# Agent attention with a gated convolution on one core: the 49th agent's weight written as one minus the other 48

## The chip, the cores and the metric

The kernel runs on one NeuronCore of a Trainium2 chip. The metric is device time in microseconds (us) of one execution, the median of several runs. The core has five engines that run side by side, each through its own list of instructions in order: TensorE (PE, matrix products; PEld is its loading of weights), VectorE (DVE), ScalarE (ACT), GpSimd (POOL) and SyncE (SP). In this kernel SP issues every DMA but one.

## What is computed

Four batches of 12800 tokens with 128 channels, and 49 agents in each batch:

```python
a2k = softmax(scale * agents @ k.T); agent_v = a2k @ v        # 49 x 128
q2a = softmax(scale * q @ agents.T);  x = q2a @ agent_v       # 12800 x 128
gate = sigmoid(sum over 5 taps of conv_w[k] * x shifted by 4 - k tokens)   # zeros ahead of a batch
out = (gate * (x @ w_val)) @ w_out
```

Every row of `q2a` holds 49 weights that add up to one. The inputs are random, and the agents, q, k and the convolution's weights are scaled up.

## The kernel before

The tokens are taken in units of 1280; a batch has ten, and `g` counts all forty. Two units are a segment (`s` from 0 to 19), and 512 tokens are a chunk (`t` from 0 to 100, five to a segment). x itself is never formed: its product with `agent_v`, `conv_w` and `w_val` is folded into weights (`wst`, turned into `stat`) that act on the agents' softmax weights directly. For precision each weight and each softmax value is split into a 16-bit high part and a 16-bit rest, so that a product is three products: high by high, rest by high, high by rest.

**A query unit** (`queries`) goes through eight steps: scores on PE, a transpose (L400) and a maximum (L757) on DVE, the subtraction on POOL (L762), the exponential on ACT (L770), the sum and its reciprocal on DVE, the weights times 256 on DVE (L781), and then the 128 columns of the tile `pt`: the high parts by ACT (L789), a second copy of a third of the weights by POOL (L795, two instructions), and the rests by POOL (L803). There are four buffers `pt`, unit g uses buffer g modulo 4. The tile is turned by a DMA transpose (L844, SP) into rows of `x1`: 49 rows of rests, 49 rows of high parts, and 30 rows that repeat the high parts of 30 agents. The first four units are turned on PE instead.

**The third product** (high value by rest of the weight) needs each of 49 agents once more: 30 have their second copy in `x1`, and 19 are left over. For those, `shifts` (L893) copies rows of `x1` into `x2`, five times each, each copy one token further, so that all five taps of the convolution are one matrix product with 95 rows. It does that with two DMAs for a segment: 16 rows (80 rows of `x2`) and 3 rows (15 rows of `x2`). The first two segments go by single units.

**A chunk** has three parts on PE: the gate (`gates`: five products with `x1`, L931, one with `x2`, L935), the value (`values`: L958 and L962) and the output (`project`: L1003 to L1005). ACT takes the tanh (L944), DVE multiplies (L971), ACT and POOL split the result (L979, L984), ACT scales the output (L1024), SP stores two chunks at a time (L1039).

**The fold of a batch** (`fold_weights`) makes the weights from the agents' values in five steps, each a PE piece with DVE, POOL and ACT work around it: `avT` (L548 to L550) is the normalised agents' values, `gw` the same times the taps (L555), `wst` the split weights (L599 to L658), and PE's transposes of them (L669) give `stat`. The first batch's fold splits the gate's weights on ACT and POOL (L647, L636), the others on DVE (L627, L599).

**What sets the order.** PE's order is a string written out by hand (g, a and o are a chunk's gate, value and output; q, k, v, t and f the units and folds). The other engines and the DMA queue are ordered by a planner (`Plan.order`), which simulates the kernel with an estimated duration for each step and issues the steps by their simulated starts. A changed estimate or a removed step can therefore move instructions on ACT, DVE, POOL and SP. SP is one queue in order: an issue that waits for its data holds all issues behind it.

Of the kernel before, what the change touches and what calls it, by code (L numbers as in the profile page):

```python
# [31 lines left out]

NDUP = 30
THIRDS = 16
X2R = 19
LAST = 42
X2CUTS = ((0, THIRDS, 1, 3, 0.5), (THIRDS, X2R, LAST, 3, 0.2))

# [152 lines left out]
def tile_agent_attention_gated_conv(  # L191
# [335 lines left out]
    def fold_weights(b):  # L527
# [55 lines left out]

        x2g = wst[:, TAPS + 1, 0 : TAPS * X2R].rearrange("p (r k) -> p k r", k=TAPS)
        x2v = wst[:, TAPS + 2, 0 : TAPS * X2R].rearrange("p (r k) -> p k r", k=TAPS)
        ghi = wst[:, 0:TAPS, 0:A]
        vhi = wst[:, TAPS, 0:A]

        def thirds(x, first, end):
            return x[..., first:end:3]  # L590

        def lows(low, full, hi, less):


            for out, first, end in zip(low, (2, 0, 1, LAST), (A, LAST, A, A)):
                less(out, thirds(full, first, end), thirds(hi, first, end))

        def rest(out, full, s, hi):
            dve.scalar_tensor_tensor(  # L599
                out=out, in0=full, scalar=rs[:, s : s + 1], in1=hi,  # L600
                op0=ALU.mult, op1=ALU.subtract,
            )

        def val_weights():
            dve.tensor_reduce(
                out=mx[:, 1:2], in_=pv[:, 0:A], axis=AX.X, op=ALU.max,
                apply_absolute_value=True,
            )
# [6 lines left out]
            low = (  # L615
                wst[:, TAPS, 2 * A : 2 * A + THIRDS], wst[:, TAPS, 2 * A + THIRDS :],
                x2v[:, HALO, 0:THIRDS], x2v[:, HALO, THIRDS:],
            )
            lows(low, pv[:, 0:A], vhi, lambda out, full, hi: rest(out, full, 1, hi))

        gate_lows = (
            wst[:, 0:TAPS, 2 * A : 2 * A + THIRDS], wst[:, 0:TAPS, 2 * A + THIRDS :],
            x2g[:, :, 0:THIRDS], x2g[:, :, THIRDS:],
        )

        def gate_weights():
            dve.tensor_scalar_mul(ghi, gw, rs[:, 0:1])  # L627

# [5 lines left out]
        def gate_rest_pool():  # L634
            def less(out, full, hi):
                nc.gpsimd.tensor_tensor(out=out, in0=full, in1=hi, op=ALU.subtract)  # L636

            lows(gate_lows, gs, ghi, less)

        def gate_rest():  # L640
            lows(gate_lows, gw, ghi, lambda out, full, hi: rest(out, full, 0, hi))
# [10 lines left out]
        add(  # L652
            "act", 0.4,
            lambda: nc.scalar.copy(out=wst[:, 0:TAPS, A : 2 * A], in_=ghi),
            [(*w_, "g")], [(*w_, "d")],
        )
        add(
            "act", 0.22, lambda: nc.scalar.copy(out=wst[:, TAPS, A : 2 * A], in_=vhi),  # L658
            [(*w_, "v")], [(*w_, "e")],
# [83 lines left out]
    def queries(b, u):  # L743
# [30 lines left out]
        def sums():  # L774
# [47 lines left out]
    def halo(s):  # L822
# [9 lines left out]

        read.append(("x2", (s - 1) % 3, UNIT, 0))
        add("pool", 0.19, fn, read, [("x1h", s % NX)])

    def transposes(b, u):
# [36 lines left out]
        shifts(b, u)  # L873

    def shifts(b, u):

# [22 lines left out]
        if g % 2 and (g + 1) // 2 < B * NU // 2:
# [7 lines left out]
    def gates(t):  # L907
# [15 lines left out]
        xs = row_keys(segs_[0], halves_)  # L923
        x2k = [("x2", segs_[0] % 3, h, c[0]) for h in halves for c in X2CUTS]
# [26 lines left out]
    def values(t):  # L951
# [5 lines left out]
        def matmuls():  # L957
# [246 lines left out]
```

## Time and profile before

| | before |
|---|---|
| time, median of 3 runs | 419.22 us (417.06 to 420.21) |
| profiled execution, its span | 417.7 us |
| PE busy | 398.0 us, 95% |
| ACT, DVE, POOL busy | 299.7, 288.7, 243.2 us |
| moved by DMA | 127.64 MB, mean 306 GB/s |
| chain that ended last | PE 86%, DMA 5%, DVE 4%, ACT 2%, issue 1% |

The profile is of one execution more. Its own time is known as its span, from the first to the last instruction. PE's matrix products overlap and their ends are modelled, so PE's busy share says when it had work, not how well it was used; the chain of waits follows the work that ended last back from the end, and shows the pace (0.22 us for a product of 512 columns).

### The profile page before, as it was taken

Reading aid. Unit: us, or ns where it says so; the run is one execution under the profiler, and the core shown is the slowest. Engines: PE = TensorE matmul, PEld = TensorE weight load, DVE = VectorE, ACT = ScalarE, POOL = GpSimd, SP = SyncE. Lnnn points to the kernel's source line nnn. Section 1 sums busy time; section 2 is a strip of 40 time slices with the busy share of each in tenths; the row PEclk is TensorE's granted clock in tenths of the full one; section 3 lists DMA queues with packets and bytes.
Section 4 is the critical chain, followed back from the end, with each engine's and each line's share of the span. In section 5 each row is a group of like instructions: output and inputs, shape, how many; then the busy total and the mean of one; then the engine's idle time right before and its main releaser. Section 6 shows DMA issues by size and latency. Waiting matters only on the chain.

```text
span 417.7 us, 10023 instructions
## 1 busy us (share of the span) xinstructions
PE 398.0 (95%) x3905; PEld 197.6 (47%) x3905; DVE 288.7 (69%) x529; ACT 299.7 (72%) x519; POOL 243.2 (58%) x301
## 2 busy tenths in 40 slices
PE   4859999999899999999999999999999999999996
PEld 1329634446545544345546544444564544444443
DVE  3967798957747765684896876895689598745222
ACT  0647457798785767778787686788869577887775
POOL 1410447864656626656378585564178869968552
PEclk9988999999999999999999999999999999999999
DMA  8999999999999999999999999999999998974733
GB/s 314 421 416 412 370 372 318 296 351 280 303 346 315 326 297 371 259 296 371 332 355 310 275 327 346 324 315 341 316 388 288 290 316 205 268 199 143 202 128 127
DMA packets 75132, 127.64 MB, mean 306 GB/s; under 512 B 50467, under 2 KB 50851, under 8 KB 75085
## 3 DMA queue, kind: packets, MB, share of 16 engines
q1 hardware_dynamic: 74940, 126.87, 96.7%
q8 instruction: 31, 0.51, 0.5%
q10 hardware_dynamic: 144, 0.13, 0.2%
q14 instruction: 17, 0.13, 0.1%
HBM read 79.25 MB, written 26.21 MB: 253 GB/s over the span
## 4 chain that ended last, share of the span: by engine, by line
PE 86%; DMA 5%; DVE 4%; ACT 2%; issue 1%; POOL 0%; SPq 0%; DVEq 0%; ACTq 0%
PE gate L931 25%; PE sc L390 19%; PE av L494 11%; PE val L958 5%; PE out L1003 5%; DMA ld<-kT 5%; PE gate L935 5%; PE val L962 5%; PE out L1004 5%; PE out L1005 5%; ACT ob L1024 1%; PE sc L858 1%; DVE wst L599 1%; DVE h L971 1%; DVE qmx L757 0%
## 5 line engine op out<-in xcount | busy, mean ns | idle before, releaser
L984 POOL TENSOR_TENSOR hl<-h,hh 128x512 f16<-128x512 f32 x99 | 117.2, 1185 | 98.5 <-ACT hh L979 97.7
L931 PE MATMUL gate<-x,stat 128*128 128x512 f16 (+1 forms) x500 | 124.2, 378 | 0.0
L971 DVE SCALAR_TENSOR_TENSOR h<-th,val 128x512 f32<-128x512 f32 x100 | 68.0, 680 | 69.3 <-PE val L962 33.2
L390 PE MATMUL sc<-ld,ag_sb 128*32 128x320 f32 x1280 | 99.8, 448 | 8.9 <-DMA ld<-qT 6.1
L944 ACT ACTIVATE th<-gate,unscale 128x512 f32<-128x512 f32 x100 | 68.5, 685 | 21.6 <-PE gate L935 20.1
L979 ACT CAST hh<-h 128x512 f16<-128x512 f32 x99 | 60.9, 616 | 25.4 <-DVE h L971 24.5
L1024 ACT ACTIVATE ob<-out,oscale 128x512 f32<-128x512 f32 x98 | 67.4, 687 | 15.0 <-PE out L1005 14.5
L931 PEld LDWEIGHTS <-stat 128*128 128x128 f16 x505 | 48.2, 98 | 60.2 <-issue 4.8
L762 POOL TENSOR_TENSOR qw<-sT,qmx 128x490 f32<-128x490 f32 x40 | 43.0, 1076 | 41.8 <-DVE qmx L757 41.6
L390 PEld LDWEIGHTS sc<-ld,ag_sb 128*32 128x32 f32 x1280 | 38.5, 112 | 56.9 <-issue 20.0
L494 PE MATMUL av<-ld,eT 128*32 128x129 f32 (+1 forms) x1400 | 50.7, 277 | 1.7 <-DVE eT L400 1.1
L494 PEld LDWEIGHTS av<-ld,eT 128*32 128x32 f32 (+1 forms) x1400 | 45.8, 115 | 10.0 <-issue 2.9
L803 POOL TENSOR_TENSOR pt<-qw,pt 128x490 f16<-128x490 f32 x40 | 44.9, 1124 | 2.7 <-ACT pt L789 2.6
L400 DVE STREAM_TRANSPOSE sT<-sc 128x640 f32<-128x640 f32 x40 | 33.6, 843 | 16.3 <-PE sc L390 15.5
L485 ACT ACTIVATE e<-ks,kbias 128x320 f32<-128x320 f32 x80 | 39.4, 553 | 5.6 <-DVE kbias L471 2.7
L400 DVE STREAM_TRANSPOSE eT<-e 128x640 f32<-128x640 f32 x40 | 33.0, 833 | 14.2 <-ACT e L485 8.6
L795 POOL TENSOR_SCALAR pt<-qw 128x160 f16<-128x160 f32 x80 | 31.9, 418 | 16.4 <-DVE qw L781 16.4
L416 ACT COPY ks<-sc 128x640 f32<-128x640 f32 x40 | 27.6, 693 | 19.2 <-PE sc L390 17.3
L958 PE MATMUL val<-x,stat 128*128 128x512 f16 x100 | 38.0, 380 | 0.9 <-DVE wo L738 0.6
L1003 PE MATMUL out<-hh,wo 128*128 128x512 f16 x98 | 37.3, 380 | 1.0 <-ACT ob L1024 0.8
L935 PE MATMUL gate<-x,stat 95*128 95x512 f16 x100 | 38.0, 380 | 0.0
L962 PE MATMUL val<-x,stat 95*128 95x512 f16 x100 | 38.0, 380 | 0.0
(132 smaller groups left out, 401.6 us busy)
## 6 DMA issues: line engine op xcount, KB each, us to landing
ld<-qT SPq DMA_DIRECT2D x40, 640.0 KB, 10.8
ld<-kT SPq DMA_DIRECT2D x40, 640.0 KB, 8.1
ld<-vP SPq DMA_DIRECT2D x39, 645.0 KB, 7.3
outT<-ob SPq DMA_DIRECT2D x48, 512.0 KB, 6.4
x<-x SPq DMA_DIRECT2D x18, 400.0 KB, 8.2
x<-x SPq DMA_DIRECT2D x18, 75.0 KB
x<-x SPq DMA_DIRECT2D x4, 200.0 KB, 5.6
outT<-ob SPq DMA_DIRECT2D x3, 256.0 KB
```

Source lines behind the costliest of these rows:

```text
L390: nc.tensor.matmul(out=out[g * BLK : (g + 1) * BLK, j, 0:GT], lhsT=ag_sb[:, b, j * BLK : (j + 1) * BLK], rhs=src[:, g * GT : (g + 1) * GT] ...
L400: nc.vector.transpose(out=out.rearrange("p n (j i) -> p j n i", j=2), in_=in_.rearrange("p j (n i) -> p j n i", i=BLK),)
L494: nc.tensor.matmul(out=av[o + j : o + j + cols, 0 : C + 1], lhsT=et[:, n, j : j + cols], rhs=vt[:, n, :], start=(u == 0 and n < 2), stop=( ...
L931: nc.tensor.matmul(out=pg, lhsT=stat[:, k, :], rhs=x1[:, c : c + w], start=(k == 0), stop=False,)
L935: nc.tensor.matmul(out=pg, lhsT=stat[0 : TAPS * X2R, TAPS + 1, :], rhs=x2[0 : TAPS * X2R, o2 : o2 + w], start=False, stop=True,)
L944: lambda: nc.scalar.activation(out=th, in_=pg, func=AF.Tanh, scale=unscale[:, 0:1]),
L958: nc.tensor.matmul(out=pv, lhsT=stat[:, TAPS, :], rhs=x1s[(b * NCH + n0 // CH) // 5 % NX][:, PAD + o2 : PAD + o2 + w], start=True, stop=False,
L962: nc.tensor.matmul(out=pv, lhsT=stat[0 : TAPS * X2R, TAPS + 2, :], rhs=x2[0 : TAPS * X2R, o2 : o2 + w], start=False, stop=True,)
L971: lambda: nc.vector.scalar_tensor_tensor(out=h, in0=th, scalar=1.0, in1=pv, op0=ALU.add, op1=ALU.mult),
L979: "act", 0.18 + 0.43 * scale, lambda: nc.scalar.copy(out=hh, in_=h),
L984: lambda: nc.gpsimd.tensor_tensor(out=hl, in0=h, in1=hh, op=ALU.subtract),
L1024: lambda: nc.scalar.activation(out=ob[:, o : o + w], in_=po, func=AF.Copy, scale=oscale if w == CH else 1.0),
```

## The change

The softmax weights of a token add up to one, so the 49th is one minus the other 48. The changed kernel subtracts the 49th agent's value from the other 48 (a new DVE instruction in the fold) and adds the 49th agent's value times a constant one. 48 agents split evenly: 32 have their second copy in `x1` (two times 16, where it was 16 and 14), and 16 are left for `x2`, so one DMA for a segment does it and the one of three rows is gone (22 DMAs in all). The constant is ten rows of `x2` (rows 96 to 105, two for each tap: high part and rest of the weight) that hold 256, the scale of the weights. The rows are written once, at the start, by two POOL memsets and one DVE memset of 64 rows by 2560. Ahead of a batch a tap must see zero instead of one: a small tile `edge` holds the pattern, and `ones_edge` copies it into the first four columns when a segment starts a batch, and writes 256 back when the buffer is used again. The product with `x2` has 106 rows where it had 95. POOL's and ACT's tiles have 48 columns a block instead of 49.

```diff
-X2CUTS = ((0, THIRDS, 1, 3, 0.5), (THIRDS, X2R, LAST, 3, 0.2))
+R = 3 * THIRDS
+ONES = 96
+X2K = ONES + 2 * TAPS
...
+    edge = const.tile([P, HALO], F16, name="edge")
+    nc.gpsimd.memset(edge, QS)
+    nc.gpsimd.affine_select(
+        out=edge, in_=edge, pattern=[[2, HALO]], compare_op=ALU.is_ge, fill=0.0,
+        base=-ONES - 2 * HALO, channel_multiplier=1,
+    )
...
+    for t in x2s[0:2]:
+        nc.gpsimd.memset(t[AP_:, :], QS)
+    nc.vector.memset(x2s[2][AP_:, :], QS)
...
             dve.tensor_tensor(out=avT, in0=pt[:, AP_ : AP_ + A], in1=den, op=ALU.mult)
-
-        add("dve", 0.95, normalise, [at_t], ["avT"])
+            dve.tensor_scalar(
+                out=avT[:, 0:R], in0=avT[:, 0:R], scalar1=avT[:, R:A], scalar2=None,
+                op0=ALU.subtract,
+            )
+
+        add("dve", 1.05, normalise, [at_t], ["avT"])
...
-            dve.tensor_scalar_mul(vhi, pv[:, 0:A], rs[:, 1:2])
+            dve.tensor_scalar_mul(vhi, pv[:, 0:R], rs[:, 1:2])
+            dve.tensor_scalar_mul(ones_v[:, 0:1], pv[:, R:A], rs[:, 1:2])
...
         def gate_weights():
-            dve.tensor_scalar_mul(ghi, gw, rs[:, 0:1])
+            dve.tensor_scalar_mul(ghi, gw[:, :, 0:R], rs[:, 0:1])
+            dve.tensor_scalar_mul(ones_g[:, :, 0:1], gw[:, :, R:A], rs[:, 0:1])
...
-            add("act", 0.4, lambda: nc.scalar.copy(out=ghi, in_=gs), ["gs"], [(*w_, "g")])
+
+            def gate_highs():
+                nc.scalar.copy(out=ghi, in_=gs[:, :, 0:R])
+                nc.scalar.copy(out=ones_g[:, :, 0:1], in_=gs[:, :, R:A])
+
+            add("act", 0.62, gate_highs, ["gs"], [(*w_, "g")])
...
+    def ones_edge(s):
+        pairs = NU // 2
+        at = x2s[s % 3][ONES:, 0:HALO]
+        if s % pairs == 0:
+            add("pool", 0.1, lambda: nc.gpsimd.tensor_copy(out=at, in_=edge[ONES:, :]), (), [("x2e", s % 3)])
+        elif s >= 3 and (s - 3) % pairs == 0:
+            add("pool", 0.1, lambda: nc.gpsimd.memset(at, QS), (), [("x2e", s % 3)])
...
-        for r0, r1, first, every, us in X2CUTS:
-            first += A
-            rows = x1[first : first + 1 + (r1 - r0 - 1) * every : every, c : c + 1]
...
+        rows = x1[R + 1 : 2 * R : 3, c : c + 1]
+        view = [rows.ap[0], (1, TAPS), (1, n * UNIT)]
+        add(
+            "dma", 0.6,
+            lambda: nc.sync.dma_start(
+                out=x2[0 : TAPS * THIRDS, o : o + n * UNIT],
+                in_=bass.AP(rows.tensor, rows.offset, view),
+            ),
+            src, [("x2", s % 3, o + i * UNIT) for i in range(n)], 0.55 * n, urge=4.0 * (g < SINGLE),
+        )
+        if g % 2 == (n == 2):
+            ones_edge(s)
...
-                out=pg, lhsT=stat[0 : TAPS * X2R, TAPS + 1, :],
-                rhs=x2[0 : TAPS * X2R, o2 : o2 + w], start=False, stop=True,
+                out=pg, lhsT=stat[0 : X2K, TAPS + 1, :],
+                rhs=x2[0 : X2K, o2 : o2 + w], start=False, stop=True,
```

PE's list of instructions is the same, instruction by instruction. On the other engines the planner has moved some. The largest move is around segment 4 (units 8 and 9, the last of batch 0). In the built program before, SP's list there reads as follows; `x1_0` receives units 8 and 9, `x1_1` units 11 and 10, `pt1` is unit 9's tile, `pt3` unit 11's, `pt2` unit 10's, and `x21` is the buffer of segment 4.

```order
L383 DMA ld10_71<-kT 128x1280
L844 DMA_TRANSPOSE x1_0_101<-pt1_98 128x10x128
L383 DMA ld0_61<-vP 128x1290
L383 DMA ld1_62<-vP 128x1290
L1039 DMA outT<-ob1_121 128x1024
L893 DMA x21_106<-x1_0_101 80x1x2560
L893 DMA x21_106<-x1_0_101 15x1x2560
L1039 DMA outT<-ob2_122 128x1024
L844 DMA_TRANSPOSE x1_1_102<-pt3_100 128x10x128
L1039 DMA outT<-ob3_123 128x1024
L844 DMA_TRANSPOSE x1_1_102<-pt2_99 128x10x128
```

In the built program of the change the same stretch of SP's list, with the line numbers of the changed kernel (L394 loads, L868 transposes, L925 shifts, L1073 stores):

```order
L394 DMA ld10_71<-kT 128x1280
L394 DMA ld0_61<-vP 128x1290
L394 DMA ld1_62<-vP 128x1290
L1073 DMA outT<-ob1_121 128x1024
L1073 DMA outT<-ob2_122 128x1024
L868 DMA_TRANSPOSE x1_1_102<-pt3_100 128x10x128
L868 DMA_TRANSPOSE x1_0_101<-pt1_98 128x10x128
L1073 DMA outT<-ob3_123 128x1024
L868 DMA_TRANSPOSE x1_1_102<-pt2_99 128x10x128
L925 DMA x21_106<-x1_0_101 80x1x2560
L394 DMA ld2_63<-kT 128x1280
```

Unit 9's transpose now stands behind unit 11's and behind two stores, and segment 4's shift stands behind the transposes of units 11 and 10, which it does not need. A move on POOL goes with it. POOL's list there before is (L803 is the last step of a unit's tile, L984 a chunk's split):

```order
L795 TENSOR_SCALAR pt1_98<-qw1_90 128x10x16
L795 TENSOR_SCALAR pt1_98<-qw1_90 128x10x14
L984 TENSOR_TENSOR hl0_117<-h0_111,hh0_114 128x512
L803 TENSOR_TENSOR pt1_98<-qw1_90,pt1_98 128x10x49
L984 TENSOR_TENSOR hl1_118<-h1_112,hh1_115 128x512
L762 TENSOR_TENSOR qw2_91<-sT0_85,qmx0_87 128x10x49
L984 TENSOR_TENSOR hl2_119<-h2_113,hh2_116 128x512
L984 TENSOR_TENSOR hl0_117<-h0_111,hh0_114 128x512
L762 TENSOR_TENSOR qw1_90<-sT1_86,qmx1_88 128x10x49
```

and in the program of the change (L819, L827, L786 and L1018 are the lines of L795, L803, L762 and L984; L905 is the new `edge` copy):

```order
L819 TENSOR_SCALAR pt1_98<-qw1_90 128x10x16 x2
L1018 TENSOR_TENSOR hl0_117<-h0_111,hh0_114 128x512
L1018 TENSOR_TENSOR hl1_118<-h1_112,hh1_115 128x512
L786 TENSOR_TENSOR qw2_91<-sT0_85,qmx0_87 128x10x49
L905 COPY x22_107<-edge_161 32x4
L1018 TENSOR_TENSOR hl2_119<-h2_113,hh2_116 128x512
L1018 TENSOR_TENSOR hl0_117<-h0_111,hh0_114 128x512
L827 TENSOR_TENSOR pt1_98<-qw1_90,pt1_98 128x10x48
L786 TENSOR_TENSOR qw1_90<-sT1_86,qmx1_88 128x10x49
```

The last step of unit 9's tile has moved from behind the first split to behind the fourth.

## Rows read from the trace of the kernel before

**Rows 1.** The page: the span, the busy time of each engine, and the chain that ended last, by engine.

```profile
span 417.7 us, 10023 instructions
...
PE 398.0 (95%) x3905; PEld 197.6 (47%) x3905; DVE 288.7 (69%) x529; ACT 299.7 (72%) x519; POOL 243.2 (58%) x301
...
PE 86%; DMA 5%; DVE 4%; ACT 2%; issue 1%; POOL 0%; SPq 0%; DVEq 0%; ACTq 0%
```

**Rows 2.** Busy time of each engine by stretches: from and to, length, then PE, PEld, DVE, ACT and POOL busy (instructions), the granted TensorE clock, the DMA share and GB/s.

```profile
0.00:24.50 24.50, 15.61 (x180) 6.36 (x184) 16.94 (x38) 8.85 (x14) 8.18 (x18) 1.00 0.93 374
...
60.00:412.00 352.00, 348.98 (x3328) 169.06 (x3321) 244.93 (x432) 268.48 (x464) 226.15 (x267) 1.00 0.98 295
```

**Rows 3.** The chain that ended last in order of time: start, length, what.

```profile
2.62 8.04 DMA ld<-kT
10.74 13.58 DMA ld<-kT
...
138.94 0.22 PE gate L931
...
236.55 1.83 DVE wst L599 x4
...
240.74 0.50 DVE wst L599 x3
```

**Rows 4.** Who waited for whom: the longest wait of PE for a load that is not the first one (in total, times, longest).

```profile
PE sc L390 <- DMA ld<-kT: 2.1, 3, 1.5
```

**Rows 5.** Groups by line and shape (rows x columns): the gate's products with 128 rows and with 95; busy time, mean ns of one, idle time before.

```profile
L931 PE MATMUL gate<-x,stat 128*128 128x512 f16 x495 | 123.3, 379 | 0.0
...
L935 PE MATMUL gate<-x,stat 95*128 95x512 f16 x99 | 37.7, 381 | 0.0
```

**Rows 6.** DMA: all packets, and the shifts from `x1` to `x2` by size (times, KB each, median us from issue to landing where known).

```profile
DMA packets 75132, 127.64 MB, mean 306 GB/s; under 512 B 50467, under 2 KB 50851, under 8 KB 75085
...
x<-x SPq DMA_DIRECT2D x18, 400.0 KB, 8.2
x<-x SPq DMA_DIRECT2D x18, 75.0 KB
...
x<-x SPq DMA_DIRECT2D x4, 37.5 KB
```

**Rows 7.** The line of the shifts: SP's time for an issue (ns, min/median/max), and from issue to landing.

```profile
L893 SPq DMA_DIRECT2D x<-x x44: 625/763/1107, 43.9 to 392.3; - x44
...
DMA to landing us min/median/max: 5.6/8.1/9.9
```

**Rows 8.** The timeline of the start on DVE and POOL: start, length, instruction, and in brackets the idle time before it and what ended it.

```profile
1.76 0.56 POOL L285 MEMSET wst<- 128x256 f16 x2
...
4.45 0.50 DVE L310 TENSOR_SCALAR ob<-ob 128x261 int32<-128x261 int32 x2 [2.79 <-DMA ob<-moe]
...
10.16 1.02 POOL L762 TENSOR_TENSOR qw<-sT,qmx 128x490 f32<-128x490 f32 x1 [7.84 <-DVE qmx L757]
```

**Rows 9.** Groups by line and shape: small instructions of the fold on DVE, and POOL's small memset.

```profile
L609 DVE TENSOR_SCALAR mx<-mx 128x1 f32<-128x1 f32 x4 | 0.6, 154 | 0.1
...
L599 DVE SCALAR_TENSOR_TENSOR wst<-av,rs,wst 128x3 f16<-128x3 f32 x3 | 0.7, 218 | 0.0
...
L548 DVE TENSOR_SCALAR den<-av 128x49 f32<-128x49 f32 x3 | 0.6, 205 | 0.1
...
L825 POOL MEMSET x<- 128x4 f16 x3 | 0.3, 105 | 0.0
```

**Rows 10.** The timeline of the first batch's fold on ACT and PE.

```profile
49.70 0.41 ACT L647 CAST wst<-gs 128x245 f16<-128x245 f32 x1 [1.07 <-POOL gs L630]
50.14 0.40 ACT L654 COPY wst<-wst 128x245 f16<-128x245 f16 x1
50.44 0.23 ACT L658 COPY wst<-wst 128x49 f16<-128x49 f16 x1
...
51.02 0.78 PE L669 MATMUL gate<-ident,wst 128*128 128x128 f16 x8
```

**Rows 11.** The timeline around segment 4, from the lists of SP, POOL, ACT and PE.

```profile
114.83 5.58 SPq L844 DMA_TRANSPOSE x<-pt  x1
...
124.56 1.48 SPq L893 DMA_DIRECT2D x<-x  x2
...
132.22 2.15 SPq L844 DMA_TRANSPOSE x<-pt  x1
...
113.70 1.11 POOL L803 TENSOR_TENSOR pt<-qw,pt 128x490 f16<-128x490 f32 x1
...
119.76 1.17 POOL L984 TENSOR_TENSOR hl<-h,hh 128x512 f16<-128x512 f32 x1 [1.47 <-ACT hh L979]
...
127.05 1.12 POOL L803 TENSOR_TENSOR pt<-qw,pt 128x490 f16<-128x490 f32 x1
...
129.94 0.59 ACT L789 CAST pt<-qw 128x490 f16<-128x490 f32 x1
...
138.99 0.38 PE L935 MATMUL gate<-x,stat 95*128 95x512 f16 x1
```

**Rows 12.** The line of the DMA transposes: SP's time for an issue (ns, min/median/max), and from issue to landing.

```profile
L844 SPq DMA_TRANSPOSE x<-pt x36: 1351/2936/7727, 62.1 to 386.9; - x36
...
DMA to landing us min/median/max: 3.9/6.9/10.1
```

More of the change, by code (lines that the diff above doesn't have):

```diff
@@ L582, in fold_weights @@
         )
[L584 to L590, printed above, removed]
+        x2g = wst[:, TAPS + 1, 0 : TAPS * THIRDS].rearrange("p (r k) -> p k r", k=TAPS)
+        x2v = wst[:, TAPS + 2, 0 : TAPS * THIRDS].rearrange("p (r k) -> p k r", k=TAPS)
+        ones_g = wst[:, TAPS + 1, ONES:X2K].rearrange("p (k t) -> p k t", t=2)
+        ones_v = wst[:, TAPS + 2, X2K - 2 : X2K]
+        ghi = wst[:, 0:TAPS, 0:R]
+        vhi = wst[:, TAPS, 0:R]
         def lows(low, full, hi, less):
-            for out, first, end in zip(low, (2, 0, 1, LAST), (A, LAST, A, A)):
-                less(out, thirds(full, first, end), thirds(hi, first, end))
+            for out, first in zip(low, (2, 0, 1)):
+                less(out, full[..., first:R:3], hi[..., first:R:3])
         def rest(out, full, s, hi):
@@ L613, in val_weights @@
             dve.reciprocal(out=rs[:, 1:2], in_=mx[:, 1:2])
[L614 removed]
+            dve.tensor_scalar_mul(vhi, pv[:, 0:R], rs[:, 1:2])
+            dve.tensor_scalar_mul(ones_v[:, 0:1], pv[:, R:A], rs[:, 1:2])
             low = (
[L616 to L619 removed]
+                wst[:, TAPS, 2 * R : 2 * R + THIRDS], wst[:, TAPS, 2 * R + THIRDS :],
+                x2v[:, HALO, :],
+            )
+            lows(low, pv[:, 0:R], vhi, lambda out, full, hi: rest(out, full, 1, hi))
+            rest(ones_v[:, 1:2], pv[:, R:A], 1, ones_v[:, 0:1])
         gate_lows = (
[L622 to L623 removed]
+            wst[:, 0:TAPS, 2 * R : 2 * R + THIRDS], wst[:, 0:TAPS, 2 * R + THIRDS :], x2g,
         )
         def gate_weights():
[L627 removed]
+            dve.tensor_scalar_mul(ghi, gw[:, :, 0:R], rs[:, 0:1])
+            dve.tensor_scalar_mul(ones_g[:, :, 0:1], gw[:, :, R:A], rs[:, 0:1])
         def gate_scaled():
@@ L636, in less @@
                 nc.gpsimd.tensor_tensor(out=out, in0=full, in1=hi, op=ALU.subtract)
-            lows(gate_lows, gs, ghi, less)
+            lows(gate_lows, gs[:, :, 0:R], ghi, less)
+            less(ones_g[:, :, 1:2], gs[:, :, R:A], ones_g[:, :, 0:1])
         def gate_rest():
-            lows(gate_lows, gw, ghi, lambda out, full, hi: rest(out, full, 0, hi))
+            lows(gate_lows, gw[:, :, 0:R], ghi, lambda out, full, hi: rest(out, full, 0, hi))
+            rest(ones_g[:, :, 1:2], gw[:, :, R:A], 0, ones_g[:, :, 0:1])
         w_ = ("wst", x)
@@ L653, in fold_weights @@
             "act", 0.4,
-            lambda: nc.scalar.copy(out=wst[:, 0:TAPS, A : 2 * A], in_=ghi),
+            lambda: nc.scalar.copy(out=wst[:, 0:TAPS, R : 2 * R], in_=ghi),
             [(*w_, "g")], [(*w_, "d")],
@@ L657, in fold_weights @@
         add(
-            "act", 0.22, lambda: nc.scalar.copy(out=wst[:, TAPS, A : 2 * A], in_=vhi),
+            "act", 0.22, lambda: nc.scalar.copy(out=wst[:, TAPS, R : 2 * R], in_=vhi),
             [(*w_, "v")], [(*w_, "e")],
@@ L781, in queries @@
             lambda: nc.vector.scalar_tensor_tensor(
-                out=w, in0=e, scalar=QS, in1=r.unsqueeze(2).to_broadcast([P, NBLK, A]),
+                out=w, in0=w, scalar=QS, in1=r.unsqueeze(2).to_broadcast([P, NBLK, R]),
                 op0=ALU.mult, op1=ALU.mult,
@@ L788, in queries @@
         add(
-            "act", 0.6, lambda: nc.scalar.copy(out=pt[:, :, A : 2 * A], in_=w),
+            "act", 0.6, lambda: nc.scalar.copy(out=pt[:, :, R : 2 * R], in_=w),
             [("qw", g % NPT)], [(*p_, 0)],
@@ L793, in again @@
         def again():
-            for o, end, first, last in ((2 * A, 2 * A + THIRDS, 2, A), (2 * A + THIRDS, P, 0, LAST)):
+            for o, first in ((2 * R, 2), (2 * R + THIRDS, 0)):
                 nc.gpsimd.tensor_scalar(
-                    out=pt[:, :, o:end], in0=w[:, :, first:last:3],
+                    out=pt[:, :, o : o + THIRDS], in0=w[:, :, first::3],
                     scalar1=1.0, scalar2=0.0, op0=ALU.mult, op1=ALU.add,
@@ L803, in queries @@
             lambda: nc.gpsimd.tensor_tensor(
-                out=pt[:, :, 0:A], in0=w, in1=pt[:, :, A : 2 * A], op=ALU.subtract
+                out=pt[:, :, 0:R], in0=w, in1=pt[:, :, R : 2 * R], op=ALU.subtract
             ),
@@ L831, in halo @@
             read = [(x, (s - 1) % NX, 1) for x in ("x1", "x1b")]
-        read.append(("x2", (s - 1) % 3, UNIT, 0))
+        read.append(("x2", (s - 1) % 3, UNIT))
         add("pool", 0.19, fn, read, [("x1h", s % NX)])
@@ L923, in gates @@
         xs = row_keys(segs_[0], halves_)
-        x2k = [("x2", segs_[0] % 3, h, c[0]) for h in halves for c in X2CUTS]
+        x2k = [("x2", segs_[0] % 3, h) for h in halves] + [("x2e", segs_[0] % 3)]
         st = [("stat", x, 0), ("stat", x, 1)]
@@ L962, in matmuls @@
             nc.tensor.matmul(
-                out=pv, lhsT=stat[0 : TAPS * X2R, TAPS + 2, :],
-                rhs=x2[0 : TAPS * X2R, o2 : o2 + w], start=False, stop=True,
+                out=pv, lhsT=stat[0 : X2K, TAPS + 2, :],
+                rhs=x2[0 : X2K, o2 : o2 + w], start=False, stop=True,
             )
```

15 lines of the change are left out of this document (2 added, 13 removed).

## The prediction

> **What bounds the kernel now.** I read the page first, then busy time by stretches, then the chain that ended last, and at last the waits. The page shows PE busy for 398.0 of 417.7 us, and a chain that is 86% PE [rows 1]. [...] Before 24.5 us it is different: PE is busy 15.6 us and the chain consists of the loads of k, 8.04 and 13.58 us [rows 2, 3]. That is 21.6 us, which is the whole 5% that the chain has for DMA [rows 1]; after it the chain has none, and SP's queue has 0%. The longest total that PE waited for a load other than the first is 2.1 us [rows 4]. The other parts of the chain are short pieces of DVE and ACT, most visibly in the fold of batch 2 (236 to 241 us) [rows 3].
>
> So PE's own work sets the end from about 60 us on, and PE's list is the same before and after. The change can win only what PE still waits, and lose what it makes PE wait.
>
> **The change part by part.**
>
> *The 22 DMAs that go.* SP spends 0.763 us on an issue of this line [rows 7]: 22 x 0.763 = 16.8 us of SP's time. The bytes are 18 x 75.0 + 4 x 37.5 = 1500 KB, 1.5 of 127.64 MB, or 1.2% [rows 6]. What hides this today is PE's work: the DMA engines are busy 0.98 of the time from 60 to 412 us, yet PE stands still for 3.0 us in 352 [rows 2]. I take 0. The other end is the whole 3.0 us. Were the cover gone and the span followed the bytes, 1.2% of 417.7 would be 5.0 us.
>
> *The product with x2 on 106 rows for 95.* A product with 128 rows takes 379 ns, one with 95 rows 381 ns [rows 5]. The rows between cost nothing: 0.
>
> *48 for 49 columns in a query unit; 16 for 14 in the second copy.* Some 2% less on ACT, DVE and POOL instructions of about 1 us or less, none of which is on the chain for long: 0, under PE's work.
>
> *The memsets at the start.* A POOL memset of 256 columns takes 0.56 / 2 = 0.28 us [rows 8]; ten times that, 2.8 us, is my upper price for 2560 columns on either engine, since it also multiplies the fixed part. POOL is free from 1.76 + 0.56 = 2.3 us to 10.16 us [rows 8], and two memsets with the small ones need about 6.2 us, so it is done at 8.5. DVE has 2.79 us idle ahead of 4.45 us [rows 8], just the price of one. Cost 0. If POOL needed twice as long, its first subtraction would come 4 us later, for a unit whose shift is issued at 43.9 us [rows 7]: still 0.
>
> *The edges.* Eight POOL instructions of about 0.1 us [rows 9], on an engine that is 58% busy [rows 1]. Those that reuse a buffer wait for the value products of three segments earlier. In POOL's list they stand next to splits (L1018) of the same or later chunks, which wait for the same products. Cost 0.
>
> *The fold.* On DVE a subtraction (like L548, 0.205 us) and two scalings of a few elements (0.154 to 0.218 us) are new [rows 9]; the rests stay four and four. That is 0.6 us of DVE for each of batches 1 to 3. In batch 0 it is the subtraction, and on ACT a small copy, 0.23 us by L658 [rows 10], ahead of L654. There ACT is ready at 50.67 and PE begins the transposes (L669) at 51.02 [rows 10]: 0.35 us of room. The subtraction moves PE's product with `avT` by 0.2 and all behind it, ACT's copies come 0.43 later. Both together: between 0.2 and 0.45 us, I take 0.3. For batch 2, where the chain runs through this DVE work [rows 3], between 0 and 0.6: I take 0.4, nearer the upper end for that reason. Batches 1 and 3 have the same bounds, and the chain is not there: 0. Sum 0.7, bounds 0.2 and 2.3.
>
> *Unit 9 and the shift of segment 4.* Before, unit 9's tile was complete at 113.70 + 1.11 = 114.81 us, its transpose went out at 114.83, and the shift at 124.56, 14.4 us ahead of the product that reads it, at 138.99 [rows 11]. In the new lists the tile's last step stands behind the split that ends at 119.76 + 1.17 = 120.93, so it ends at 122.04. The shift also stands behind the transpose of unit 10, whose tile is complete at 127.05 + 1.12 = 128.17 [rows 11]. SP's time for a transpose is 1.35, 2.94 or 7.73 us (least, median, most) [rows 12], so the shift goes out at 129.5, 131.1 or 135.9. From there to landing it is 5.6, 8.1 or 9.9 us [rows 7]: it lands at 135.1, 139.2 or 145.8. At the medians that is 0.2 us behind 138.99, and the gate itself is 0.3 later by the fold: 0. The bounds are 0 and 145.8 - 139.3 = 6.5 us. I take 0, also because SP now issues less in the microseconds ahead, so the queue is shorter than at the median. Behind the late shift stand the next loads, which go out at about 132 us; before, SP reached them after the transpose of 132.22 [rows 11], so they lose nothing. A second wait hangs on unit 9: unit 13 uses the same tile, and its ACT step at 129.94 [rows 11] needs unit 9's transpose landed, at 122.04 + 6.9 = 128.9 (10.1: 132.1) [rows 12]. Behind that step on ACT stand the chunks' splits and tanh, for which PE waits. At the median 0, at worst 2.2 us.
>
> **Sum.** 0 + 0 + 0 + 0 + 0 + 0.7 + 0 = 0.7 us on the profiled execution's 417.7: 418.4. The runs shown have a median of 419.22, 1.5 above it, so on their scale 419.9 us.
>
> **The rivals.**
>
> *Segment 4 is late (slower).* Place: the gate product of chunk 20 at 138.99. Price: each microsecond that the shift lands behind 139.3 is lost, since PE has nothing else in its list. It makes the kernel slower by over 1% from a landing at 143.5 on. With the longest issue of a transpose and the median landing, 135.9 + 8.1 = 144.0, the loss is 4.7 and the time 424.6; at the far end 6.5 and 426.4. For it: the medians already meet the edge. Against it: both long values belong to a full DMA queue, and here SP waits for POOL with little outstanding. 0.13.
>
> *The DMA engines are the hidden bound (faster).* They are busy 0.98 of the time [rows 2]. If the span followed the bytes, 419.2 - 5.0 = 414.2 us. [...] 0.06. [...]
>
> *No measurable effect,* my forecast: 0.81.
>
> **How the numbers follow.** About 1% (4.2 us) is what a measurement of this kernel can tell from no change; its three runs lie within 3.2 us. Forecast 419.9. The low end is 419.9 less the 3.0 us that PE stands still, 416.9, rounded out to 416.5; the high end is the late segment at 424.6. That leaves out the DMA rival and the far end of the late one, with what I don't see: about 2 in 10. Faster by over 1%: 0.06; slower by over 1%: 0.13; within: 0.81.
>
> **What the profile after would show.** Right: the chain at 85 to 87% PE with no DMA after 25 us; PE busy about 349 of 352 us in the middle; SP with 22 issues fewer; the fold's DVE pieces 0.6 us longer; segment 4's shift issued near 131 us, and no idle time of PE ahead of that gate product. Wrong: PE waiting there for a DMA x<-x (first rival), or the first 60 us or the middle shorter by several us with PE's pieces unchanged (second), or waits of PE on ACT or POOL where the planner moved an instruction that I have not followed.

## The result, and the profile after

The changed kernel takes 421.03 us (median of 20 runs, 419.75 to 423.54), the kernel before, in runs beside it, 419.11 us (416.75 to 420.94). The medians lie 1.9 us apart. The ratio over all runs is 1.0056, 95% interval 1.0037 to 1.0076, which is 1.6 to 3.2 us slower: inside the bound of 1% and inside the forecast range, with the sign that was forecast. Forecast were 0.7 us. The profiled execution took 419.75 us, 1.75 more than its span.

The page of the changed kernel, where [rows 1], [rows 5] and [rows 6] show the kernel before:

```profile
span 418.0 us, 10025 instructions
...
PE 397.1 (95%) x3905; PEld 196.5 (47%) x3905; DVE 295.9 (71%) x541; ACT 299.1 (72%) x520; POOL 249.4 (60%) x313
...
DMA packets 74735, 126.11 MB, mean 302 GB/s; under 512 B 50400, under 2 KB 50784, under 8 KB 74688
...
PE 84%; DMA 8%; DVE 5%; ACT 1%; issue 1%; SPq 0%; DVEq 0%
...
L969 PE MATMUL gate<-x,stat 106*128 106x512 f16 x100 | 38.0, 380 | 0.0
...
x<-x SPq DMA_DIRECT2D x18, 400.0 KB, 6.6
```

The bytes fell by 1.5 MB, the shift of 16 rows lands in 6.6 us instead of 8.2, and PE is busy as long as before. The busy time in the middle stretch, against 348.98 in [rows 2]:

```profile
60.00:412.00 352.00, 347.81 (x3309) 168.24 (x3302) 245.87 (x439) 267.33 (x463) 226.05 (x274) 1.00 0.95 290
```

PE lost 1.2 us there at the same granted clock (1.00 in both). The chain in order of time says where; before it ran through the fold of batch 2 [rows 3], now it runs through that of batch 1 too:

```profile
140.78 0.67 DVE h L1005
142.40 1.08 DVE wst L643
143.48 0.58 DVE h L1005
144.06 2.00 DVE wst L613 x4
146.99 0.56 DVE wst L613 x4
147.60 0.61 PE av L692 x8
```

L643 scales five numbers a row and takes 1.08 us, where [rows 9] have 0.15 to 0.22 for such instructions. The timeline of that fold on DVE, POOL and PE shows what ran beside it (start, length):

```profile
139.82 1.03 DVE L562 TENSOR_SCALAR avT<-avT 128x48 f32<-128x48 f32 x1
...
142.12 0.37 DVE L642 TENSOR_SCALAR wst<-gw,rs 128x240 f16<-128x240 f32 x1
142.40 1.08 DVE L643 TENSOR_SCALAR wst<-gw,rs 128x5 f16<-128x5 f32 x1
...
143.99 2.07 DVE L613 SCALAR_TENSOR_TENSOR wst<-gw,rs,wst 128x80 f16<-128x80 f32 x4
...
139.66 1.15 POOL L1018 TENSOR_TENSOR hl<-h,hh 128x512 f16<-128x512 f32 x1 [1.08 <-ACT hh L1013]
...
142.18 1.27 POOL L1018 TENSOR_TENSOR hl<-h,hh 128x512 f16<-128x512 f32 x1 [0.64 <-ACT hh L1013]
143.41 1.06 POOL L827 TENSOR_TENSOR pt<-qw,pt 128x480 f16<-128x480 f32 x1
144.85 1.19 POOL L1018 TENSOR_TENSOR hl<-h,hh 128x512 f16<-128x512 f32 x1 [0.38 <-ACT hh L1013]
...
142.74 1.24 PE L965 MATMUL gate<-x,stat 128*128 128x512 f16 x5 [0.64 <-ACT th L978]
...
147.60 0.61 PE L692 MATMUL av<-ident,wst 128*128 128x128 f16 x8 [0.73 <-DVE wst L613]
```

The subtraction L562 ends at 140.85 and POOL's split beside it at 140.81; L643 ends at 143.48 and POOL's at 143.45. These two DVE instructions, whose operands all lie in SBUF, end within 0.04 us of POOL's. POOL's side shows a smaller difference: its split at 142.18, which began 0.06 us behind L642, took 1.27 us, the one at 139.66 took 1.15.

In the kernel before the same place reads (timeline):

```profile
144.38 0.94 DVE L599 SCALAR_TENSOR_TENSOR wst<-gw,rs,wst 128x80 f16<-128x80 f32 x4
...
144.14 0.18 POOL L828 COPY x<-x 128x4 f16<-128x4 f16 x1
145.25 1.16 POOL L984 TENSOR_TENSOR hl<-h,hh 128x512 f16<-128x512 f32 x1 [0.93 <-ACT hh L979]
...
147.35 0.61 PE L669 MATMUL av<-ident,wst 128*128 128x128 f16 x8
```

The four rests took 0.94 us with POOL nearly idle; now they take 2.07, since the planner has put a unit's last step (L827) between two splits. PE, which waited for nothing here, now waits twice: 0.73 us ahead of the transposes, and 0.64 us ahead of a gate product at 142.74. That one starts with the subtraction: behind it DVE's product (`h`, L1005) comes late, and behind that ACT's tanh, for which PE waits.

### The profile page after: what moved, and what is told of

Same layout as the page of the kernel before. It is cut to its first block, busy times and chain, and to the rows that moved or that the text cites. A ratio compares the mean times of both kernels' runs of the same rounds, so it can differ in the third digit from the quotient of the medians.

```text
span 418.0 us, 10025 instructions
## 1 busy us (share of the span) xinstructions
PE 397.1 (95%) x3905; PEld 196.5 (47%) x3905; DVE 295.9 (71%) x541; ACT 299.1 (72%) x520; POOL 249.4 (60%) x313
## 4 chain that ended last, share of the span: by engine, by line
PE 84%; DMA 8%; DVE 5%; ACT 1%; issue 1%; SPq 0%; DVEq 0%
PE gate L965 24%; PE sc L401 18%; PE av L505 11%; DMA ld<-kT 5%; PE val L992 5%; PE out L1037 5%; PE gate L969 5%; PE val L996 5%; PE out L1038 5%; PE out L1039 4%; DMA ld<-vP 3%; DVE h L1005 1%; DVE wst L613 1%; PE sc L882 1%; DVE eT L411 0%
## 5 line engine op out<-in xcount | busy, mean ns | idle before, releaser
L1018 POOL TENSOR_TENSOR hl<-h,hh 128x512 f16<-128x512 f32 x99 | 117.8, 1192 | 96.7 <-ACT hh L1013 89.5
L1005 DVE SCALAR_TENSOR_TENSOR h<-th,val 128x512 f32<-128x512 f32 x100 | 67.9, 679 | 64.9 <-PE val L996 34.4
L786 POOL TENSOR_TENSOR qw<-sT,qmx 128x490 f32<-128x490 f32 x40 | 43.3, 1084 | 33.5 <-DVE qmx L781 33.3
L505 PE MATMUL av<-ld,eT 128*32 128x129 f32 (+1 forms) x1400 | 49.6, 275 | 1.1 <-DVE qr L800 0.6
L505 PEld LDWEIGHTS av<-ld,eT 128*32 128x32 f32 (+1 forms) x1400 | 44.7, 114 | 9.5 <-issue 3.1
L827 POOL TENSOR_TENSOR pt<-qw,pt 128x480 f16<-128x480 f32 x40 | 43.3, 1086 | 3.1 <-ACT pt L813 3.1
L819 POOL TENSOR_SCALAR pt<-qw 128x160 f16<-128x160 f32 x80 | 32.5, 424 | 21.2 <-DVE qw L805 8.2
L969 PE MATMUL gate<-x,stat 106*128 106x512 f16 x100 | 38.0, 380 | 0.0
L996 PE MATMUL val<-x,stat 106*128 106x512 f16 x100 | 38.0, 380 | 0.0
```

The lines of the kernel that those rows point to most:

```text
L505: nc.tensor.matmul(out=av[o + j : o + j + cols, 0 : C + 1], lhsT=et[:, n, j : j + cols], rhs=vt[:, n, :], start=(u == 0 and n < 2), stop=( ...
L969: nc.tensor.matmul(out=pg, lhsT=stat[0 : X2K, TAPS + 1, :], rhs=x2[0 : X2K, o2 : o2 + w], start=False, stop=True,)
L996: nc.tensor.matmul(out=pv, lhsT=stat[0 : X2K, TAPS + 2, :], rhs=x2[0 : X2K, o2 : o2 + w], start=False, stop=True,)
L1005: lambda: nc.vector.scalar_tensor_tensor(out=h, in0=th, scalar=1.0, in1=pv, op0=ALU.add, op1=ALU.mult),
L1018: lambda: nc.gpsimd.tensor_tensor(out=hl, in0=h, in1=hh, op=ALU.subtract),
```

## The experiments

Two explanations were open: the instructions that the change adds to the fold wait for POOL, or the planner's new order costs the time by itself. Beside the ratio, each profiled execution gives the length of each fold, in us. Fold 0 runs from the first product of batch 0's fold (L536) to the first gate product. The others are taken between the starts of products with `x2`, of the chunk of a segment that comes first in PE's order: fold 1 from segment 4 to 5, fold 2 from 8 to 10, fold 3 from 14 to 15. "3 to end" leaves out the first 115 us, which differ by up to 3.7 us between single executions. Stretches without a fold agree far better: from segment 5 to 7 all 14 profiles take 33.65 us. Below the first row stand differences to the kernel before.

| kernel | ratio to before, 95% interval | fold 0 | fold 1 | fold 2 | fold 3 | 3 to end |
|---|---|---|---|---|---|---|
| before | 1 | 7.07 | 17.21 | 31.83 | 14.61 | 300.9 |
| the change | 1.0056 [1.0037, 1.0076] | +0.24 | +1.93 | +0.55 | +0.05 | +2.1 |
| e1 change, order of before | 1.0043 [1.0011, 1.0075] | +0.25 | +1.07 | +0.55 | +0.06 | +1.0 |
| e2 before, order of the change | 1.0065 [1.0038, 1.0092] | 0 | +1.08 | 0 | 0 | +1.7 |
| e3 change, no fold extras | 0.9978 [0.9954, 1.0002] | -0.16 | +0.22 | -0.50 | 0 | -0.3 |
| e4 change, small transfers back | 1.0103 [1.0055, 1.015] | +0.24 | +1.94 | +0.55 | +0.06 | +3.2 |
| e5 subtraction from PSUM | 1.0049 [1.0026, 1.0072] | +0.46 | +1.36 | -0.08 | +0.28 | +1.2 |
| e6 all fold extras from PSUM | 1.0099 [1.0065, 1.0134] | +0.47 | +2.39 | -0.22 | +0.67 | +3.1 |
| e7 as e6, order of before | 1.0036 [1.0007, 1.0065] | +0.47 | +0.74 | -0.22 | +0.66 | +0.8 |
| e8 as e3, order of before | 0.9978 [0.9954, 1.0001] | -0.16 | +0.24 | -0.50 | 0 | -0.8 |
| e9 before, no small transfers | 0.9987 [0.9967, 1.0007] | 0 | 0 | +0.01 | 0 | -0.5 |
| e10 best of the change | 1.0027 [1.0003, 1.0052] | +0.48 | +0.70 | +0.21 | +0.55 | +0.9 |
| e11 before + subtraction, SBUF | 1.0101 [1.008, 1.0122] | +0.58 | +0.93 | +0.51 | +1.81 | +3.4 |
| e12 before + subtraction, PSUM | 1.0017 [0.9985, 1.0049] | +0.18 | +0.17 | 0 | +0.05 | +0.3 |

The last column ranks the kernels nearly as the ratios do. For the change the four folds add up to 2.8 us, inside the 1.6 to 3.2 us of its ratio; for every run but e2 the sum lies inside the run's interval. So what the change costs is lost in the folds.

**Order and work apart.** e1 gives the planner the old estimates and a step that issues nothing in place of the removed transfer, so all lists keep the order of before:

```diff
-        add("dve", 1.05, normalise, [at_t], ["avT"])
+        add("dve", 0.95, normalise, [at_t], ["avT"])
...
+        add(
+            "dma", 0.6, lambda: None,
+            src, [("x2s", s % 3, o + i * UNIT) for i in range(n)], 0.2 * n, urge=4.0 * (g < SINGLE),
+        )
```

> All of the change's work, but the planner is told of a second DMA step without an instruction and of the old durations, so that ACT, DVE, POOL and SP keep the order of the kernel before. If the loss (ratio 1.0056, some 2 us) comes from the fold's new DVE instructions that wait for POOL (theory A), the time stays near that of the change: ratio 1.003 to 1.007, and in the profile the subtraction in the fold takes about 1 us where POOL is at work. If it comes from the instructions that the planner moved, unit 9 and segment 4 above all (theory B), the time is that of the kernel before: 0.998 to 1.002.

e2 is the reverse, the work of before with the change's estimates, both transfers of a segment in one step and an empty step for the edges:

```diff
-        add("dve", 0.95, normalise, [at_t], ["avT"])
+        add("dve", 1.05, normalise, [at_t], ["avT"])
...
+            add("pool", 0.1, lambda: None, (), [("x2e", s % 3)])
...
+            "dma", 0.6, both, src,
```

> The work of the kernel before, with both DMAs of a segment in one step of the planner and the changed durations, so that ACT, DVE, POOL and SP have the order of the changed kernel. Theory A: ratio 0.998 to 1.002, since the fold is the old one. Theory B: 1.003 to 1.008.

e3 is the change without what it adds to the fold, so that its output lacks the 49th agent's part:

```diff
-            dve.tensor_scalar(
-                out=avT[:, 0:R], in0=avT[:, 0:R], scalar1=avT[:, R:A], scalar2=None,
-                op0=ALU.subtract,
-            )
...
-            dve.tensor_scalar_mul(ones_g[:, :, 0:1], gw[:, :, R:A], rs[:, 0:1])
...
-            rest(ones_g[:, :, 1:2], gw[:, :, R:A], 0, ones_g[:, :, 0:1])
```

> The changed kernel without the fold's new instructions: no subtraction and no weights for the rows of ones (they stay zero), so the 49th agent's part is left out of the output. Theory A: the loss goes, ratio 0.997 to 1.002, and the gate products of batch 1 and 2 start 1 to 2 us and about 0.5 us earlier against the chunks ahead of them. Theory B: 1.004 to 1.007, as the change.

e4 puts the 22 transfers of three rows back, into rows of `x2` whose weights are zero:

```diff
+            nc.sync.dma_start(
+                out=x2[TAPS * THIRDS : TAPS * THIRDS + 15, o : o + n * UNIT],
+                in_=bass.AP(three.tensor, three.offset, view3),
+            )
```

> The changed kernel in its order, with the 22 DMAs of three rows issued again behind those of 16 rows, into rows of x2 whose weights are zero. If the removed DMAs are hidden under PE's work, as forecast, the ratio stays that of the change, 1.004 to 1.008. If their removal wins 1 us or more somewhere (start, segment 4), it is 1.008 or above.

Neither explanation stands alone. In the fold of batch 1 the additions cost 1.1 us in the old order (e1), the order costs 1.1 us with the old work (e2), and the new order without the additions 0.2 (e3). PE's two waits part in the same way: in e1 it waits only ahead of the gate (0.64 us), in e2 only ahead of the transposes (0.91). e2's timeline shows the order's part at work, on instructions that are as old as the kernel before:

```profile
145.04 2.52 DVE L599 SCALAR_TENSOR_TENSOR wst<-gw,rs,wst 128x80 f16<-128x80 f32 x4
...
144.80 1.09 POOL L803 TENSOR_TENSOR pt<-qw,pt 128x490 f16<-128x490 f32 x1
145.91 1.16 POOL L993 TENSOR_TENSOR hl<-h,hh 128x512 f16<-128x512 f32 x1
...
149.08 0.61 PE L669 MATMUL av<-ident,wst 128*128 128x128 f16 x8 [0.91 <-DVE wst L599]
```

So both look like the same wait: DVE at POOL's side, for added instructions (L562 1.03 us, L643 1.08) or for old ones that the order puts beside POOL (the four rests 2.52 us, 0.94 in the kernel before). e4's folds are those of the change, and its loss against it has another place. Its PE timeline:

```profile
139.20 0.39 PE L977 MATMUL gate<-x,stat 106*128 106x512 f16 x1 [0.45 <-DMA x<-x]
...
403.93 0.39 PE L977 MATMUL gate<-x,stat 106*128 106x512 f16 x1 [0.31 <-DMA x<-x]
```

These are the products that read the shifts of segments 4 and 19, which the new order issues late. The transfers of 16 rows had landed, at 137.49 and 402.87; PE waits for those of three rows, issued behind them.

**Where the added instructions read.** e5 lets the subtraction read PSUM, at the price of one instruction more:

```diff
+            dve.tensor_tensor(
+                out=pt[:, 4 * AP_ : 4 * AP_ + R], in0=pt[:, AP_ : AP_ + R], in1=den[:, 0:R],
+                op=ALU.mult,
+            )
             dve.tensor_scalar(
-                out=avT[:, 0:R], in0=avT[:, 0:R], scalar1=avT[:, R:A], scalar2=None,
-                op0=ALU.subtract,
+                out=avT[:, 0:R], in0=pt[:, 4 * AP_ : 4 * AP_ + R], scalar1=avT[:, R:A],
+                scalar2=None, op0=ALU.subtract,
             )
```

> The changed kernel with one step of the fold written otherwise: the quotient is put into PSUM, the 49th column apart into SBUF, and the subtraction reads PSUM. That is one DVE instruction more in each fold (about 0.2 us), and every engine's order is otherwise that of the changed kernel. Theory 'port': a DVE instruction that reads only SBUF ends no earlier than the POOL instruction that runs beside it, and one that reads PSUM doesn't wait; then the subtraction is 0.2 to 0.3 us in all four folds, where it was 1.03 us in three of them, and the fold of batch 1 loses about 0.6 us less, since the scaling of five and one rest still wait there: ratio to the kernel before about 1.004. Theory 'number': an added DVE instruction costs its own time and its wait for the one before it, whatever it reads; then this kernel is 0.2 us a fold slower than the changed one, ratio 1.006 to 1.007.

e6 adds the same for the five gate weights, whose product ACT puts into PSUM; e7 is e6 in the order of before.

```diff
+                lambda: nc.scalar.activation(
+                    out=go, in_=conv_sb.unsqueeze(2), func=AF.Copy, scale=avT[:, R:A]
+                ),
...
-            dve.tensor_scalar_mul(ones_g[:, :, 0:1], gw[:, :, R:A], rs[:, 0:1])
+            dve.tensor_scalar_mul(ones_g[:, :, 0:1], go, rs[:, 0:1])
```

> As the kernel with the subtraction from PSUM, and in batches 1 to 3 the five gate weights of the 49th agent come from PSUM too: ACT puts their product with the 3x3 kernel there (one ACT instruction of about 0.2 us a fold), and DVE's scaling and rest of them read it there. So nothing that the change adds to DVE reads only SBUF. Theory 'port': what the additions cost in batch 1 goes, but the order of the changed kernel keeps the rests of the 48 beside POOL's instructions: ratio 1.001 to 1.004. Theory 'number': 1.006 to 1.008, for it has two instructions more a fold.

> The same additions that read PSUM, in the order of the kernel before. If the change's loss is the sum of two parts, what its additions wait at POOL's side and what its order makes the fold of batch 1 wait, both are gone here: ratio 0.995 to 1.000, and the fold of batch 1 takes what it took before within 0.3 us. If the additions cost by their number, about 1.004, as with the change's own additions in the old order.

The line of the subtraction (ns, min/median/max), in the change and then in e5:

```profile
L562 DVE TENSOR_SCALAR avT<-avT x4: 247/639/1091, 47.0 to 335.1; 128x48 f32<-128x48 f32 x4
```

```profile
L568 DVE TENSOR_SCALAR avT<-av,avT x3: 268/268/268, 142.7 to 336.9; 128x48 f32<-128x48 f32 x3
```

From SBUF it took 0.25 us in batches 0 and 3 and 1.03 and 1.09 in batches 1 and 2 (two of four, where the expectation above has three). From PSUM it took 0.27 us each time, and batch 1's fold is 0.6 us shorter although it has one instruction more. The ratio moved little, within its interval. e6 went against the expectation: 1.0099. Its added instructions wait for nothing (0.22 us each), but DVE now reaches the old rests just as POOL begins L843, and they take the wait; its DVE and PE timeline:

```profile
143.90 2.57 DVE L629 SCALAR_TENSOR_TENSOR wst<-gw,rs,wst 128x80 f16<-128x80 f32 x3
...
146.55 0.42 PE L609 MATMUL av<-avT,moe_sb 128*128 128x49 f32 x2 [1.78 <-DVE wst L629]
```

In e7, in the old order, the same three take 0.90 us:

```profile
144.04 0.90 DVE L629 SCALAR_TENSOR_TENSOR wst<-gw,rs,wst 128x80 f16<-128x80 f32 x3
```

The fold of batch 1 is then 1.6 us shorter than in e6, which is the order's price alone. e7 missed its expected 0.995 to 1.000: with more instructions the folds of batches 0, 1 and 3 stay 0.5, 0.7 and 0.7 us longer.

**What the removal is worth.** e8 is e3 with the empty step and the old estimates of e1. e9 takes only the transfers out of the kernel before:

```diff
-                lambda r0=r0, r1=r1, rows=rows, view=view: nc.sync.dma_start(
+                lambda r0=r0, r1=r1, rows=rows, view=view: None if r0 else nc.sync.dma_start(
...
-                out=pg, lhsT=stat[0 : TAPS * X2R, TAPS + 1, :],
+                out=pg, lhsT=stat[0 : TAPS * THIRDS, TAPS + 1, :],
```

> The change's transfer, memsets and 48 columns in the order of the kernel before, without the subtraction and without the 49th agent's weights (its part is missing in the output). It prices the removal of the 22 small transfers with the memsets and edges alone. If the removed transfers were worth nothing, as predicted: ratio 0.999 to 1.001. If they hold back other transfers (the run with them back in the new order was at 1.010): 0.993 to 0.997.

> The kernel before without its 22 transfers of three rows; the products with x2 read 80 rows in place of 95 (the rows that these transfers fill have no part in the output). Every other instruction stands as in the kernel before. The prediction priced the removal at nothing, at most 3.0 us. What the traces so far say: where the shift of a segment goes out early, the second transfer delays nothing that PE waits for; the run with the small transfers back lost its time where the new order made the shifts of segments 4 and 19 late. Then the ratio is 0.998 to 1.001. Were the transfers a load on the queues or on SBUF that slows all else, as that run's 1.010 would also allow: 0.992 to 0.996.

e9 is 0.13% below before, and its interval holds 1. Without them the shift of 16 rows lands in 6.8 us (median) instead of 8.2, and PE's gates come no earlier. e8's 0.9978 lies between its two expectations; its gain lies in the folds of batch 2 (0.50 us), which has three rests for four, and batch 0 (0.16).

**One instruction alone.** e10 is e1 with e5's subtraction and the five-weight scaling moved behind the rests:

```diff
         def gate_rest():
...
+            dve.tensor_scalar_mul(ones_g[:, :, 0:1], gw[:, :, R:A], rs[:, 0:1])
             rest(ones_g[:, :, 1:2], gw[:, :, R:A], 0, ones_g[:, :, 0:1])
```

> The change's work in the order of the kernel before, the subtraction reading PSUM, and the scaling of the 49th agent's five gate weights put behind the rests of the 48, so that ACT adds nothing and one DVE instruction that reads SBUF stands at a later place. If the fold's loss is what waits at POOL: about 0.5 us behind the kernel before in the fold of batch 1 and level elsewhere, ratio 0.998 to 1.002, below 1.0036 of the kernel with an ACT instruction more a fold. If the number of DVE instructions counts: 1.003 to 1.005.

It is the fastest complete version of the change, still not faster than the kernel before, and just above its expected 1.002: the last rest of five weights meets POOL's next split and takes 1.09 us. e11 adds to the kernel before nothing but the subtraction, into a tile that nobody reads; e12 differs from it in one operand:

```diff
+            dve.tensor_scalar(
+                out=spare[:, 0 : A - 1], in0=avT[:, 0 : A - 1], scalar1=avT[:, A - 1 : A],
+                scalar2=None, op0=ALU.subtract,
+            )
```

```diff
-                out=spare[:, 0 : A - 1], in0=avT[:, 0 : A - 1], scalar1=avT[:, A - 1 : A],
+                out=spare[:, 0 : A - 1], in0=pt[:, AP_ : AP_ + A - 1], scalar1=avT[:, A - 1 : A],
```

> The kernel before with one DVE instruction more in each fold, the subtraction, at the same place as in the change, written to a spare tile that nothing reads; everything else and every order as before. Price of the prediction: 0.2 us a fold, of which the folds of batches 0 and 2 were to show some: ratio 1.000 to 1.001. If the instruction waits for POOL: it takes about 1.0 us in batches 0 to 2, and the fold of batch 1 ends 0.6 to 1.0 us later: ratio 1.001 to 1.004.

> As the kernel before with one DVE subtraction more a fold, at the same place, of the same size and also written to the spare tile, but its tensor input is in PSUM (the agents' sums) in place of SBUF. The run with SBUF was at 1.0101 and its instruction took 1.02 to 1.15 us in all four folds. If what costs is the wait of an instruction that reads only SBUF beside a POOL instruction: 0.27 us each, the folds of batches 1 to 3 end 0.1 to 0.4 us later, ratio 1.000 to 1.003. If it is the place in DVE's list, whatever is read: 1.008 to 1.012.

The line in e11 and, from the timeline of batch 3's fold, what follows it:

```profile
L552 DVE TENSOR_SCALAR spare<-avT x4: 686/1057/1147, 46.9 to 334.5; 128x48 f32<-128x48 f32 x4
```

```profile
337.97 1.84 DVE L604 SCALAR_TENSOR_TENSOR wst<-gw,rs,wst 128x80 f16<-128x80 f32 x4
...
338.37 1.16 POOL L989 TENSOR_TENSOR hl<-h,hh 128x512 f16<-128x512 f32 x1 [2.24 <-ACT hh L984]
...
341.91 0.38 PE L963 MATMUL val<-x,stat 128*128 128x512 f16 x1 [1.65 <-DVE h L976]
```

From batch 1's fold in e11, the gate that waits as in the change:

```profile
142.39 1.24 PE L936 MATMUL gate<-x,stat 128*128 128x512 f16 x5 [0.64 <-ACT th L949]
```

And the line in e12:

```profile
L552 DVE TENSOR_SCALAR spare<-av,avT x3: 267/267/267, 141.4 to 335.1; 128x48 f32<-128x48 f32 x3
```

With the same place, size and order, the operand's memory decides: 0.27 us against 1.02 to 1.15 in batches 1 to 3 (0.69 in batch 0, beside a shorter POOL instruction), 1.0017 against 1.0101. In batch 1 e11 has the change's wait of 0.64 us ahead of the gate, and e12 has none. The wait also displaces what stands behind it: in batch 3 the rests then meet the next split and PE waits 1.65 us; e11 lies above both its expectations. One subtraction of 48 columns a fold costs 3.4 us from segment 3 on, more than the whole change. That it costs more alone than in the change fits its length in batch 3, where it was 0.25 us in the change (335.14, POOL's split only at 335.34) and 1.15 in e11.

## Why the prediction was right, and where its size was off

- **The bound, and no effect of the transfers: right.** PE's list sets the end. e9 prices the 22 DMAs at nothing that its interval tells from none, within the 3.0 us allowed. A span that followed the bytes would have been 5.0 us shorter; nothing of that size showed: the interval of e9 reaches at most 1.4 us below the kernel before. In the change's order they would cost, as e4 shows, because that order leaves those of two segments no room.
- **106 rows, memsets, edges: right.** 380 ns for 106 rows. Two memsets took POOL 4.55 us, priced at 5.6.
- **The fold: right sign, mis-sized.** 0.7 us were taken, as 0.3, 0, 0.4 and 0 for batches 0 to 3, with bounds of 0.2 and 2.3. The folds cost 0.24, 1.93, 0.55 and 0.05, together 2.8. The term that failed is batch 1's, for two reasons. The price of the subtraction came from rows that read PSUM (L548, and L599 from `av`, [rows 9]); from SBUF it took 1.03 us there, and the new scaling of five 1.08. And the term was set to 0 because the chain did not run there; with these waits, and with the rests that the new order puts beside L827, it does. Batch 2's near hit is in part luck: the additions cost 1.05 us (e1 against e8), on a fold that had become 0.5 shorter.
- **48 for 49 columns at 0: not quite.** The gate weights' scaling fell from 0.47 to 0.37 us in the change's fold of batch 1, but beside a split it took 1.24 in e8 (last section).
- **Segment 4: 0 was right, the margin was not the forecast's.** The shift went out at 131.03, forecast 131.1, and PE's product had no wait:

```profile
117.67 10.58 SPq L868 DMA_TRANSPOSE x<-pt  x2
...
131.03 1.26 SPq L925 DMA_DIRECT2D x<-x  x1
...
130.35 0.59 ACT L813 CAST pt<-qw 128x480 f16<-128x480 f32 x1 [2.00 <-DMA x<-pt]
...
130.43 0.81 POOL L819 TENSOR_SCALAR pt<-qw 128x160 f16<-128x160 f32 x2 [3.96 <-DMA x<-pt]
...
137.31 0.38 PE L969 MATMUL gate<-x,stat 106*128 106x512 f16 x1
```

  But in this execution PE was 1.7 us ahead of [rows 11], and the transposes of units 11 and 9 ahead of it took SP 10.58 us together, of the long kind that the prediction held for unlikely here: 6.28 us were left from issue to product. In the trace of before the longest transpose, 7.73 us at 86.21, had seven issues of SP in the 8 us ahead of it; of the four shifts whose landing is known there, the one that landed after 9.9 us had six, the one after 5.6 one. Here the longer of the two transposes, 7.95 us, had four, the other transpose among them. The shift landed after 5.63, the short end of [rows 7]; at the median of 8.1 PE would have waited 1.8 us. In each profile with the change's order the shift of 16 rows landed after 5.5 to 5.8 us, which the prediction did not know. The second wait on unit 9's transpose came as described, 2.00 us on ACT and 3.96 on POOL, and cost PE nothing. e4's 0.45 us is the first rival's mechanism, at its edge.
- **The test "no DMA in the chain after 25 us": wrong.** The chain takes in a load of `vP`, 10.66 us from 183.90, yet PE's longest wait for a load behind 25 us is 0.10 us, at 194.56. A share of the chain is no loss by itself.
- **What would make it wrong** was named: PE waiting "where the planner moved an instruction that I have not followed". It was POOL's L827 in batch 1's fold; the profile puts PE's waits down to DVE and ACT, which came late behind it and behind the subtraction.

Open: e2's ratio puts it 1.6 to 3.9 us behind the kernel before, and its folds explain 1.1; its single profile can't place the rest. No version that computes the whole output beat the kernel before beyond its interval.

## What to carry to other kernels

Price a small DVE instruction by what it reads and by what POOL runs beside it: here a row taken with POOL idle (the subtraction in batch 0 of the change, 0.25 us) or from PSUM (0.27 us) was a lower bound, and the upper one was about the length of POOL's instruction (1.02 to 1.24 us, beside splits of 1.16). A planner whose costs hold no such pairs can lose by a neutral move what an edit gains. Of two equal forms, the one that read PSUM kept its length of 0.27 us in all four folds (e5, e12).

## What the runs showed of the hardware that was not expected

With one column less a block the gate weights' scaling took up to 1.24 us. The line in the kernel before, all three at one length, the one at 143.11 beside a POOL split from 143.03:

```profile
L627 DVE TENSOR_SCALAR wst<-gw,rs x3: 467/472/474, 143.1 to 336.6; 128x245 f16<-128x245 f32 x3
```

and in e8, the one at 142.12 beside a split from 142.04:

```profile
L636 DVE TENSOR_SCALAR wst<-gw,rs x3: 361/370/1243, 142.1 to 335.0; 128x240 f16<-128x240 f32 x3
```

So 0.08 us behind the start of a split the form of 245 columns took 0.47 us and that of 240 took 1.24. No run varied the shape alone, so the cause was not shown.

At the start, beside POOL's two memsets, the first two bit operations on `ob` took 2.90 us, where they took 0.50 in [rows 8]; they ended at 7.44, the memsets at 7.29.

```profile
2.74 4.55 POOL L295 MEMSET x<- 64x2560 f16 x2
...
4.54 2.90 DVE L321 TENSOR_SCALAR ob<-ob 128x261 int32<-128x261 int32 x2
```
